# Attention heads turned another way: every second head of the last three chunks token-major, and the late modulation weights summed during the first output projection

## The chip, the cores and the metric

One NeuronCore of one Trainium2 chip runs the whole program. The metric is device time in microseconds (us) of one execution; less is better. The engines are named as the profile names them: PE is TensorE's matmul, PEld its weight load, DVE VectorE, ACT ScalarE, POOL GpSimd, SP the sync engine, which issues most DMAs. "SPq" and "ACTq" are rows of DMA issues on the queues of SP and ACT.

## The reference

One transformer layer with adaptive layer norm: 2048 tokens, width 1024, 32 query heads of 128 on 4 key/value heads, of whose 2048 keys only the last 512 are seen, and a gated FFN of width 3584. All tensors are bf16.

```
mod = silu(c) @ w_mod                      -> six rows of 1024: sa, ca, ga, sb, cb, gb
h = layernorm(x) * (1 + ca) + sa
q = h @ wq;  s = q k^T / sqrt(128)         # k, v: the last 512 positions of the caches
o = softmax(s) @ v;  x = x + ga * (o @ wo)
h = layernorm(x) * (1 + cb) + sb
x = x + gb * ((silu(h @ w_gate) * (h @ w_up)) @ w_down)
```

## The kernel before

**Tiling.** The tokens are four chunks of 512 (`CH`), each of four tiles of 128. Attention runs chunk by chunk, 32 heads in each, so 128 heads in all, numbered `i`; after the last head of a chunk comes that chunk's output projection, `oproj` (eight pieces `k` of 32 matmuls, in turn into PSUM banks `QB` and `XB`); the last chunk's is spread over the loop's end. The FFN follows, chunk by chunk. Layer norms are generators (`ln_task`) that `run_bg` advances one step per head; their DMA turns put the normalized rows feature-major into `hT`.

**Order.** One recording layer, `T.op` (L55), emits every instruction in program order and adds the semaphore waits that its buffers need, so each engine runs its instructions in the order of the loop at L903, and a wait holds up all that stands behind it on its engine. Nearly every matmul has line L271.

**One head before.** In iteration `i` stand: `qproj(i+3)`, eight 128x512 matmuls into bank `QB`, which DVE copies to a `qT` slot (CAST, L644); `scores(i-1)`, four 128x512 matmuls with the keys stationary, so that a score tile has keys on its partitions, into banks 0 to 3, and two `Exp` of 1024 columns on ACT (L813) into one of two `ex` slots; `pv(i-2)`, sixteen 128x129 matmuls with a piece of the probabilities stationary and the values moving, their 129th column a column of ones that gives the row sums, into banks 5 and 6. DVE then takes the reciprocals (L831), scales the 128x512 result (L834), and SP turns it by DMA (L837, "o-turn" below) into the head's row of `oT_all`, which `oproj` reads. SP also loads 1 MB of `wq` for every four heads (`load_wq`, L357).

**The late weights.** 24 columns of `mod` (sb, cb and gb) are wanted only in the FFN. `load_mt(n)` (L588) loads 128 columns of `w_mod` turned by DMA, `mod_col(n)` (L593) multiplies them by silu(c) and sums along the row on DVE. Before, one of each stands at every 9/4 heads from head 34 on, through chunk 1 and into chunk 2, with two buffers.

**Names.** `resid` (L853, L855) multiplies a finished PSUM bank by the gate and adds it to `x_res`, both on DVE; `oproj_end` calls it. `mod_take` and `mod_gain` copy finished columns to where `modulate` reads them.

Of the kernel before, what the change touches and what calls it, by code (L numbers as in the profile page):

```python
# [3 lines left out]
ALU = mybir.AluOpType  # L4
AF = mybir.ActivationFunctionType
BF16 = mybir.dt.bfloat16
# [124 lines left out]
def bass_adaLN_cond__sliding_block_cached__swiglu_ffn__prompt_kernel(  # L131
# [44 lines left out]
    def dq(name, issuer=None):  # L176
        return T.stream(name, nc.alloc_semaphore(name), issuer or nc.sync, inc=16)
# [44 lines left out]
    def bank(b, n=512, off=0):  # L222
        return ps[:, b * 512 + off:b * 512 + off + n]
# [19 lines left out]
    B_mv = [_Buf("mv%d" % i) for i in range(4)]  # L243
    B_rs = [_Buf("rs%d" % i) for i in range(4)]
    B_rl = [_Buf("rl%d" % i) for i in range(2)]
    B_ns = [_Buf("ns%d" % i) for i in range(2)]
    B_tmp = [_Buf("tmp%d" % i) for i in range(2)]
    B_h2 = [[_Buf("h2_%d_%d" % (s, dt)) for dt in range(DT)] for s in range(2)]
# [12 lines left out]
    with nc.Block() as block:  # L261

        @block.gpsimd
        def _(g):
# [5 lines left out]
            def mm(out_ap, lhsT, rhs, start, stop, reads, bank_buf, skip=False):  # L270
                T.op(PE, lambda: TE.matmul(out_ap, lhsT, rhs, start=start, stop=stop, skip_group_check=skip),  # L271
                     reads=reads, writes=[bank_buf])
# [145 lines left out]


            B_ns4 = B_ns + [_Buf("ns2"), _Buf("ns3")]  # L420
            nsc4 = [t[:, :] for t in nsc] + [arena.at(OFF_EX + (4 + 2 * i) * KB, [D], BF16, [B_ns4[2 + i]]) for i in range(2)]
# [154 lines left out]

            NF = NE + DT
            NL = NJ - NF
            B_mt = [_Buf("mt%d" % i) for i in range(2)]
            mt = [arena.at(OFF_H20 + (2 + 2 * i) * KB, [D], BF16, [B_mt[i]]) for i in range(2)]  # L580
            sc_row = arena.at(OFF_H20 + 6 * KB, [D], BF16, [B_scr])
            Q_mt = [dq("q_mt%d" % i) for i in range(2)]

            def load_mt(n):
                if n < 2:
                    for b_ in B_qT[NQT:]:
                        B_mt[n].absorb(b_)
                T.op(Q_mt[n % 2], lambda: SP.dma_start_transpose(  # L588
                    mt[n % 2].rearrange("p (a b) -> p a b", a=1), w_mod[:, (NF + n) * P:(NF + n + 1) * P]),
                     writes=[B_mt[n % 2]])  # L590

            def mod_col(n):
                T.op(DVE, lambda: V.scalar_tensor_tensor(mt[n % 2], mt[n % 2], 1.0, sc_row, op0=ALU.mult, op1=ALU.mult,  # L593
                                                         accum_out=mcol[:, n:n + 1]),
                     reads=[B_scr], writes=[B_mt[n % 2], B_mcol])
# [150 lines left out]
            for dt in range(DT):  # L746
                shift(dt)

            B_ex = [_Buf("ex%d" % i) for i in range(NEX)]
            ex_s = [arena.at(OFF_EX + i * 4 * KB, [KT, CH], BF16, [B_ex[i]]) for i in range(NEX)]  # L750
# [54 lines left out]
            def scores(i):  # L805
                ch, h = divmod(i, Hq)
                gk = h // rep
                qs = q_slot(i)
                es = i % NEX
                for kt in range(KT):  # L810
                    mm(bank(SCB + kt), kT_sb[:, gk * KT + kt, :], qT_s[qs], True, True, [B_kT[gk], B_qT[qs]], PB[SCB + kt])
                for kp in range(KT // 2):
                    T.op(ACT, lambda: A.activation(ex_s[es][:, 2 * kp:2 * kp + 2, :], banks2(SCB + 2 * kp), AF.Exp, scale=att_scale),  # L813
                         writes=[PB[SCB + 2 * kp], PB[SCB + 2 * kp + 1], B_ex[es]])

            def pv(i):
                ch, h = divmod(i, Hq)
                gk = h // rep
                es = i % NEX
                os_ = i % NOS  # L820

                for jj in range(2):
                    for kt in range(KT):
                        for jb in range(2):
                            j = 2 * jb + jj
                            b = PVB + jb
                            mm(bank(b, P + 1, jj * 130), ex_s[es][:, kt, j * P:(j + 1) * P], v_aug[:, gk * KT + kt, 0:P + 1],
                               kt == 0, kt == KT - 1, [B_ex[es], B_va, B_vg[gk]], PB[b])
                both = [PB[PVB], PB[PVB + 1]]
                r = i % 2  # L830
                T.op(DVE, lambda: V.reciprocal(rl[r][:, :].rearrange("p (a b) -> p a b", a=2), psap(PVB * 512 + P, [[512, 2], [130, 2]])),  # L831
                     writes=both + [B_rl[r]])
# [4 lines left out]
                T.op(Q_tr[os_], lambda: SP.dma_start_transpose(oT_all[:, h, :].rearrange("p (j q) -> p j q", j=TPC),  # L837
                                                               o_s[os_].rearrange("p j d -> p (j d)")),
                     reads=[B_os[os_]], writes=[B_oT[h]])

            B_wo = [_Buf("wo%d" % i) for i in range(8)]
            wo_s = [None] * 8
# [15 lines left out]
            def oproj_mm(ch, k, b, h0, h1):  # L858
                j, hf = divmod(k, 2)
                for h in range(h0, h1):  # L860
                    mm(bank(b), oT_all[:, h, j * P:(j + 1) * P], wo_s[h // 4][:, h % 4, hf * 512:(hf + 1) * 512],
                       h == 0, h == Hq - 1, [B_wo[h // 4], B_oT[h]], PB[b])
# [33 lines left out]
            t2 = Hq + 6 + (9 * (NL - 1)) // 4  # L896
            TURNT = (28, t2 + 1)
            PUTT = {33: (0, c_sil, B_csil), 30: (1, mrow[0:DT, :], B_mrow), t2 + 3: (2, mrow[0:DT, :], B_mrow)}
            GETT = {35: (0, sc_row, B_scr), 31: (1, rowb[0][:, :], B_row[0]), t2 + 4: (2, rowb[1][:, :], B_row[1])}
            LOADT = {Hq + 2 + (9 * n) // 4: n for n in range(NL)}  # L900
            LOADO = {5 + (21 * p) // 8: p for p in range(8)}
            LOADK = {1: 1, 5: 2, 6: 3}
            for i in range(1, NA + 2):  # L903
                ch, h = divmod(i, Hq)
                if i in LOADK:
# [10 lines left out]
                    load_wo(LOADO[i])  # L916
                if i in GATET:
                    gate_turn(GATET[i])
                if i in TURNT:
                    if i > Hq:  # L920
                        T.op(DVE, lambda: V.tensor_copy(mstg[:, 0:DT], mcol[:, 2 * DT:3 * DT]), reads=[B_mcol], writes=[B_mstg])
                    row_turn()
                if i in PUTT:
                    row_put(*PUTT[i])
# [8 lines left out]
                if i + LEAD < NA:  # L933
# [9 lines left out]
                        qproj_mm(NQ0 + i // 2, QB, 0, HK)  # L943
                    else:
                        qproj(NQ0 - 1 + i // 2, QB, HK)
                if i - 4 in LOADT:
                    n = LOADT[i - 4]
                    mod_col(n)
                    g0, last = divmod(n, DT)
                    if last == DT - 1:  # L950
                        mod_take(g0, B_late[g0 + 1])
                        if g0 == 1:
                            mod_gain(1, B_late[2], B_g[1])
                n = i - (NA - LEAD)
                if 0 <= n <= 2:
                    oproj_mm(NCH - 1, 0, QB, 8 * n, 8 * n + 8)
                elif n >= 3:
                    oproj_mm(NCH - 1, 1, XB, 8 * (n - 3), 8 * (n - 3) + 8)
                if 1 <= i - 1 < NA:
                    scores(i - 1)  # L960
                if 0 <= i - 2 < NA:
                    pv(i - 2)
                    ch2, h2 = divmod(i - 2, Hq)
                    if i % 4 == 1 and i > 5:
# [166 lines left out]
```

## Time and profile before

| | us |
|---|---|
| median of 3 runs | 1270.56 |
| lowest, highest | 1270.37, 1270.61 |
| the profiled execution's own time | 1270.14 |
| its span, first to last instruction | 1268.3 |
| busy: PE, PEld, DVE | 1255.1, 640.7, 485.1 |
| busy: ACT, POOL | 341.6, 56.0 |

The granted TensorE clock stands at full speed over the span. In the page's slices the DMA engines are busiest in the first tenth; over the three later chunks of attention their mean busy share lies near a half. Head stages and output projections alternate: the first `oproj` runs from 139 to 193 us, chunk 1's heads follow it, and the FFN begins near 685 us.

### The profile page before, as it was taken

How to read it: one execution, taken by the hardware profiler on the slowest of the kernel's cores; microseconds unless marked ns; L12 is line 12 of the kernel's file. 1: busy time of each engine (PE TensorE's matmuls, PEld its weight loads, DVE VectorE, ACT ScalarE, POOL GpSimd, SP SyncE). 2: the span in 40 equal slices, each digit the busy share in tenths (PEclk: the TensorE clock that was granted, in tenths of full speed). 3: DMA queues.
4: the chain of work that ended last, by engine and by line, in shares of the span. 5: the costliest groups of instructions: out<-in, count | busy, mean ns of one | idle time of the engine just before them, and what ended most of it. 6: DMA issues, size and time to landing. Idle time of an engine off the chain costs nothing.

```text
span 1268.3 us, 17609 instructions
## 1 busy us (share of the span) xinstructions
PE 1255.1 (99%) x7442; PEld 640.7 (51%) x7583; DVE 485.1 (38%) x894; ACT 341.6 (27%) x389; POOL 56.0 (4%) x95
## 2 busy tenths in 40 slices
PE   8999999999999999999999999999999999999999
PEld 5655545555455554555544444444444444444444
DVE  4676226764257641365322321233212321222122
ACT  4655205553035550155510111011100111011100
POOL 1530000000000000000000000000000000000000
PEclk9999999999999999999999999999999999999999
DMA  9998306875029641064243972055512644034200
GB/s 320 264 263 218 92 1 127 177 171 125 1 57 177 138 114 34 9 129 123 61 145 100 291 246 94 25 158 150 168 40 72 177 141 134 17 128 154 67 9 25
DMA packets 239997, 156.67 MB, mean 124 GB/s; under 512 B 133296, under 2 KB 225840, under 8 KB 239920
## 3 DMA queue, kind: packets, MB, share of 16 engines
q1 hardware_dynamic: 181664, 96.83, 31.6%
q10 hardware_dynamic: 58256, 58.73, 14.6%
q8 instruction: 59, 0.97, 0.3%
q14 instruction: 18, 0.15, 0.1%
HBM read 119.93 MB, written 4.20 MB: 98 GB/s over the span
## 4 chain that ended last, share of the span: by engine, by line
PE 98%; issue 1%; DMA 0%; SPq 0%; DVE 0%
PE ps L271 98%; DMA arena<-in_w_mod_dram 0%; SPq L309 0%; SPq L334 0%; PE ps L275 0%; DVE arena L496 0%; DVE tmp L853 0%; DVE arena L855 0%; DVE gain_f L486 0%
## 5 line engine op out<-in xcount | busy, mean ns | idle before, releaser
L271 PE MATMUL ps<-arena 128*128 128x512 bf16 (+1 forms) x7213 | 1249.3, 333 | 10.1 <-POOL arena L298 2.0
L271 PEld LDWEIGHTS ps<-arena 128*128 128x128 bf16 x7354 | 632.9, 98 | 621.5 <-issue 2.1
L813 ACT ACTIVATE arena<-ps 128x1024 bf16<-128x1024 f32 x256 | 261.9, 1023 | 345.1 <-PE ps L271 333.4
L1059 ACT ACTIVATE arena<-ps 128x512 bf16<-128x512 f32 x112 | 66.9, 597 | 499.6 <-PE ps L271 499.6
L1060 DVE TENSOR_TENSOR arena<-ps,arena 128x512 bf16<-128x512 f32 x112 | 77.5, 692 | 276.2 <-PE ps L271 276.2
L853 DVE TENSOR_TENSOR tmp<-ps,rowb 128x512 f32<-128x512 f32 (+1 forms) x65 | 44.4, 683 | 318.8 <-PE ps L271 318.8
L644 DVE CAST arena<-ps 128x512 bf16<-128x512 f32 x120 | 82.8, 690 | 47.7 <-PE ps L271 47.7
L834 DVE TENSOR_TENSOR arena<-ps,rl 128x512 bf16<-128x512 f32 x128 | 88.5, 691 | 4.7 <-DVE rl L831 0.2
L831 DVE RECIPROCAL rl<-ps 128x4 f32<-128x4 f32 x128 | 23.4, 182 | 114.1 <-PE ps L271 114.1
L429 POOL TENSOR_SCALAR rstd<-mv 128x1 f32<-128x1 f32 x28 | 6.1, 216 | 910.3 <-DVE mv L428 910.3
L424 DVE BATCH_NORM_STATS2 st<-x_res 128x6 f32<-128x512 bf16 x62 | 42.4, 683 | 3.4 <-DMA x_res<-in_A_x_dram 3.3
L593 DVE SCALAR_TENSOR_TENSOR arena<-arena 128x1024 bf16<-128x1024 bf16 x24 | 29.2, 1215 | 0.0
L855 DVE TENSOR_TENSOR arena<-tmp,x_res 128x512 bf16<-128x512 f32 (+2 forms) x33 | 22.3, 677 | 1.1
L855 DVE TENSOR_TENSOR x_res<-tmp,x_res 128x512 bf16<-128x512 f32 x32 | 22.2, 693 | 1.1
L440 DVE TENSOR_SCALAR arena<-arena,gain,mod_bf 128x512 bf16<-128x512 bf16 x56 | 21.2, 420 | 0.0
L435 DVE TENSOR_SCALAR nsc<-x_res,mv,rstd 128x1024 bf16<-128x1024 bf16 x30 | 19.2, 641 | 0.0
L431 POOL TENSOR_TENSOR rstd<-rstd,mhalf 128x1 f32<-128x1 f32 x28 | 15.7, 559 | 2.3
L772 POOL TENSOR_SCALAR arena<-arena,sc_bf 128x512 f32<-128x512 bf16 x8 | 12.9, 1614 | 0.5 <-POOL arena L774 0.2
L774 POOL TENSOR_TENSOR arena<-arena 128x512 f32<-128x512 f32 x8 | 10.1, 1265 | 0.7
L428 DVE BATCH_NORM_AGGREGATE mv<-st 128x2 f32<-128x12 f32 x28 | 5.8, 209 | 1.0
L271 PEld LDWEIGHTS ps<-sc_bf,arena 128*128 128x128 bf16 x128 | 4.4, 96 | 1.4 <-DMA arena<-in_w_mod_dram 0.3
L271 PE MATMUL ps<-sc_bf,arena 128*128 128x1 bf16 x128 | 4.7, 164 | 0.3 <-DMA arena<-in_w_mod_dram 0.3
(56 smaller groups left out, 59.4 us busy)
## 6 DMA issues: line engine op xcount, KB each, us to landing
arena<-in_A_wq_dram SPq DMA_DIRECT2D x30, 1024.0 KB, 5.8
arena<-in_B_w_gate_dram ACTq DMA_DIRECT2D x28, 1024.0 KB, 5.4
arena<-in_B_w_up_dram ACTq DMA_DIRECT2D x28, 1024.0 KB, 7.9
arena<-in_A_wo_dram SPq DMA_DIRECT2D x8, 1024.0 KB, 7.6
arena<-in_B_w_down_dram SPq DMA_DIRECT2D x7, 1024.0 KB, 8.3
out_dram<-arena SPq DMA_DIRECT2D x15, 256.0 KB, 2.0
x_res<-in_A_x_dram SPq DMA_DIRECT2D x3, 1024.0 KB, 7.0
arena<-arena SPq DMA_TRANSPOSE x132, 2.6
```

What stands on the lines that cost most here:

```text
L271: T.op(PE, lambda: TE.matmul(out_ap, lhsT, rhs, start=start, stop=stop, skip_group_check=skip), reads=reads, writes=[bank_buf])
L424: T.op(DVE, lambda: V.bn_stats(st_[sl][:, hf * 6:hf * 6 + 6], x_res[:, t, hf * 512:hf * 512 + 512]), reads=[B_x[t]], writes=[B_st[sl]])
L440: T.op(DVE, lambda: V.tensor_scalar(dst[:, dt, :], dst[:, dt, :], gain[gi][:, dt:dt + 1], mod_bf[:, ccol + dt:ccol + dt + 1], op0=ALU.mult ...
L593: T.op(DVE, lambda: V.scalar_tensor_tensor(mt[n % 2], mt[n % 2], 1.0, sc_row, op0=ALU.mult, op1=ALU.mult, accum_out=mcol[:, n:n + 1]), rea ...
L644: T.op(DVE, lambda: V.tensor_copy(qT_s[qs], bank(b)), writes=[PB[b], B_qT[qs]])
L813: T.op(ACT, lambda: A.activation(ex_s[es][:, 2 * kp:2 * kp + 2, :], banks2(SCB + 2 * kp), AF.Exp, scale=att_scale), writes=[PB[SCB + 2 * k ...
L831: T.op(DVE, lambda: V.reciprocal(rl[r][:, :].rearrange("p (a b) -> p a b", a=2), psap(PVB * 512 + P, [[512, 2], [130, 2]])), writes=both + ...
L834: T.op(DVE, lambda: V.tensor_tensor(o_s[os_].rearrange("p (a b) d -> p a b d", a=2), psap(PVB * 512, [[512, 2], [130, 2], [1, P]]), rlb, A ...
L853: T.op(DVE, lambda: V.tensor_tensor(tmp[s][:, 0:n], bank(b, n), rowb[ri][:, c0:c0 + n], ALU.mult), reads=[B_row[ri]], writes=[PB[b], B_tmp ...
L855: T.op(DVE, lambda: V.tensor_tensor(dst[:, c0:c0 + n], tmp[s][:, 0:n], x_res[:, t, c0:c0 + n], ALU.add), reads=[B_tmp[s], B_x[t]], writes= ...
L1059: T.op(ACT, lambda: A.activation(sg_s[ss], bank(gb), AF.Silu), writes=[PB[gb], B_sg[ss]])
L1060: T.op(DVE, lambda: V.tensor_tensor(guT[:, ft, :], bank(ub), sg_s[ss], ALU.mult), reads=[B_sg[ss]], writes=[PB[ub], B_gu[ft]])
```

## The change

Two things change.

**Token-major heads.** `NAT` holds the even heads from 34 to 126, 47 of them. For these, `nat_scores` makes the four query tiles stationary and moves the keys, so that a score tile has tokens on its partitions. ACT runs four `Exp` of 512 columns, each with `accum_out`, the row sum. `nat_norm` takes reciprocals of the sums on DVE, two at a time, and scales four 128x512 pieces of probabilities in place. `nat_turn` turns the whole 128x2048 tile by one DMA into a slot `pt`. `nat_pv`, four iterations later, needs four 128x512 matmuls, the values stationary and the turned probabilities moving, which give the head's result feature-major; ACT copies it to `oT_all`. Such a head has no reciprocal, no scaling and no o-turn of its own after the matmuls. Its probabilities lie in `pn[0]`, the place of `ex` slot 0, or in `pn[1]`, the place of `tmp`; the heads between use `ex` slot 1, and head 32 uses `nsc`. At a seam between chunks the first such head is placed into `oproj`: its `nat_scores` after piece 0, its `nat_norm` after piece 1.

**Late weights.** `late_cols(k)` is called behind each of the eight pieces of the first `oproj` and holds three `mod_col` each, with four buffers in the place of `hT[0]`; behind the last piece it also holds the two `mod_take` and `mod_gain`. The loop has no `mod_col` any more.

In an odd iteration the order on PE is `qproj`, `nat_scores(i+1)`, `pv(i-2)`; in an even one `qproj`, `scores(i-1)`, `nat_pv(i-4)`. `load_wq` stands one iteration earlier, ahead of `nat_turn`.

```diff
-    nsc = [S_("nsc%d" % i, [P, D], BF16) for i in range(2)]
-    tmp = [S_("tmp%d" % i, [P, 512], F32) for i in range(2)]
+    psum = [S_("psum%d" % i, [P, 4], F32) for i in range(2)]
+    pinv = [S_("pinv%d" % i, [P, 4], F32) for i in range(2)]
+    nsc_t = S_("nsc", [P, 2 * D], BF16)
+    nsc = [nsc_t[:, i * D:(i + 1) * D] for i in range(2)]
+    tmp_t = S_("tmp", [P, 1024], F32)
+    tmp = [tmp_t[:, i * 512:(i + 1) * 512] for i in range(2)]
...
+            NMT = 4
+            L_ORDER = list(range(2 * DT, NL)) + list(range(2 * DT))
+            def load_mt(m):
+                sl = m % NMT
+                n = L_ORDER[m]
+                if mt[sl] is None:
+                    mt[sl] = arena.at(OFF_HT + 2 * sl * KB, [D], BF16, [B_mt[sl]])
...
+            def late_cols(k):
+                for m in range(3 * k, 3 * k + 3):
+                    mod_col(m)
+                    if m + NMT < NL:
+                        load_mt(m + NMT)
+                if k == 3:
+                    T.op(DVE, lambda: V.tensor_copy(mstg[:, 0:DT], mcol[:, 2 * DT:3 * DT]), reads=[B_mcol], writes=[B_mstg])
+                    row_turn()
+                if k == 4:
+                    row_put(2, mrow[0:DT, :], B_mrow)
+                if k == 5:
+                    row_get(2, rowb[1][:, :], B_row[1])
+                if k == 7:
+                    for g0 in range(2):
+                        mod_take(g0, B_late[g0 + 1])
+                    mod_gain(1, B_late[2], B_g[1])
...
+            NAT0 = Hq + 2
+            NAT = set(range(NAT0, NA, 2))
+            B_pn = [[_Buf("pn0_%d" % hf) for hf in range(2)], B_tmp]
+            pn = [None, tmp_t[:, :].bitcast(BF16)]
...
+            def ex_slot(i):
+                return NEX if i % Hq == 0 and i + 2 in NAT and i not in NAT else i % NEX
+            def p_slot(i):
+                return (i - NAT0) // 2 % 2
...
+            def nat_scores(i):
...
+                for j in range(TPC):
+                    mm(bank(SCB + j), qT_s[qs][:, j * P:(j + 1) * P],
+                       kT_sb[:, gk * KT:(gk + 1) * KT, :].rearrange("p a b -> p (a b)"), True, True,
+                       [B_kT[gk], B_qT[qs]], PB[SCB + j])
+                for j in range(TPC):
+                    T.op(ACT, lambda: A.activation(pn[s][:, j * 512:(j + 1) * 512], bank(SCB + j), AF.Exp, scale=att_scale,
+                                                   accum_out=psum[s][:, j:j + 1]),
+                         writes=[PB[SCB + j], B_pn[s][j // 2], B_psum[s][j // 2]])
+            def nat_norm(i, hf):
+                s = p_slot(i)
+                T.op(DVE, lambda: V.reciprocal(pinv[s][:, 2 * hf:2 * hf + 2], psum[s][:, 2 * hf:2 * hf + 2]),
+                     reads=[B_psum[s][hf]], writes=[B_pinv[s][hf]])
+                for j in (2 * hf, 2 * hf + 1):
+                    pj = pn[s][:, j * 512:(j + 1) * 512]
+                    T.op(DVE, lambda: V.tensor_scalar(pj, pj, pinv[s][:, j:j + 1], None, op0=ALU.mult),
+                         reads=[B_pinv[s][hf]], writes=[B_pn[s][hf]])
+            def nat_turn(i):
+                s = p_slot(i)
+                pt_of[i] = (pt[s], B_pt[s])
+                T.op(Q_pt[s], lambda: SP.dma_start_transpose(pt[s], pn[s]), reads=B_pn[s], writes=[B_pt[s]])
+            def nat_pv(i):
...
+                for kt in range(KT):
+                    mm(bank(PVB).rearrange("p (j q) -> p j q", j=TPC), v_aug[:, gk * KT + kt, 0:P], ptv[:, :, kt, :],
+                       kt == 0, kt == KT - 1, [B_va, B_vg[gk], pb], PB[PVB])
+                T.op(ACT, lambda: A.activation(oT_all[:, h, :], bank(PVB), AF.Copy), writes=[PB[PVB], B_oT[h]])
...
-            def oproj(ch):
+            def oproj(ch, between, last):
                 for k in range(2 * TPC):
                     b = [QB, XB][k % 2]
-                    oproj_mm(ch, k, b, 0, Hq)
+                    if k == 0:
+                        oproj_mm(ch, k, b, 0, Hq - 8)
+                        for n in last:
+                            nat_pv(n)
+                    oproj_mm(ch, k, b, 0 if k else Hq - 8, Hq)
                     oproj_end(ch, k, b)
+                    if k < len(between):
+                        between[k]()
+                    if ch == 0:
+                        late_cols(k)
...
-                if i - 4 in LOADT:
-                    n = LOADT[i - 4]
-                    mod_col(n)
...
+                if i % 4 == 0 and i > NAT0:
+                    load_wq(i // 4 + 2)
...
+                seam = (i - 1) % Hq == 0 and i + 1 in NAT
...
+                if i in NAT and (i - 2) % Hq:
+                    nat_norm(i, 1)
+                nat = i % 2 == 1 and i + 1 in NAT
+                if nat and not seam:
+                    run_bg(1)
+                    nat_scores(i + 1)
-                if 1 <= i - 1 < NA:
+                if 1 <= i - 1 < NA and i - 1 not in NAT:
                     scores(i - 1)
                 if 0 <= i - 2 < NA:
-                    pv(i - 2)
+                    if i - 4 in pt_of:
+                        nat_pv(i - 4)
+                    if i in NAT and (i - 2) % Hq:
+                        nat_turn(i)
+                    if i - 2 not in NAT:
+                        pv(i - 2)
+                    if nat and not seam:
+                        nat_norm(i + 1, 0)
...
                     if h2 == Hq - 1 and ch2 < NCH - 1:
-                        oproj(ch2)
-                run_bg(1)
+                        oproj(ch2, [lambda: nat_scores(i + 1), lambda: (nat_norm(i + 1, 0), nat_norm(i + 1, 1))],
+                              [n for n in sorted(pt_of) if n // Hq == ch2])
+                        if seam:
...
+                            nat_turn(i + 1)
...
-            load_wgu(0, B_oT[Hq - 2:])
-            load_wgu(1)
             HL = Hq - 4
             oproj_mm(NCH - 1, 1, XB, 16, HL)
+            for n in sorted(pt_of):
+                nat_pv(n)
+            load_wgu(0, B_oT[Hq - 1:])
+            load_wgu(1)
```

More of the change, by code (lines that the diff above doesn't have):

```diff
@@ L245, in bass_adaLN_cond__sliding_block_cached__swiglu_ffn__prompt_kernel @@
     B_rl = [_Buf("rl%d" % i) for i in range(2)]
+    B_psum = [[_Buf("psum%d_%d" % (i, hf)) for hf in range(2)] for i in range(2)]
+    B_pinv = [[_Buf("pinv%d_%d" % (i, hf)) for hf in range(2)] for i in range(2)]
     B_ns = [_Buf("ns%d" % i) for i in range(2)]
@@ L420, in _ @@
             B_ns4 = B_ns + [_Buf("ns2"), _Buf("ns3")]
-            nsc4 = [t[:, :] for t in nsc] + [arena.at(OFF_EX + (4 + 2 * i) * KB, [D], BF16, [B_ns4[2 + i]]) for i in range(2)]
+            nsc4 = nsc + [arena.at(OFF_EX + (4 + 2 * i) * KB, [D], BF16, [B_ns4[2 + i]]) for i in range(2)]
             def stats(t, sl, hf):
@@ L578, in _ @@
             NL = NJ - NF
-            B_mt = [_Buf("mt%d" % i) for i in range(2)]
-            mt = [arena.at(OFF_H20 + (2 + 2 * i) * KB, [D], BF16, [B_mt[i]]) for i in range(2)]
+            NMT = 4
+            B_mt = [_Buf("mt%d" % i) for i in range(NMT)]
+            mt = [None] * NMT
             sc_row = arena.at(OFF_H20 + 6 * KB, [D], BF16, [B_scr])
[L582 to L590, printed above, removed]
@@ L592, in mod_col @@
-            def mod_col(n):
-                T.op(DVE, lambda: V.scalar_tensor_tensor(mt[n % 2], mt[n % 2], 1.0, sc_row, op0=ALU.mult, op1=ALU.mult,
-                                                         accum_out=mcol[:, n:n + 1]),
-                     reads=[B_scr], writes=[B_mt[n % 2], B_mcol])
+            Q_mt = [dq("q_mt%d" % i) for i in range(NMT)]
+            L_ORDER = list(range(2 * DT, NL)) + list(range(2 * DT))
[4 more added lines that the diff above has]
+                    mt[sl] = arena.at(OFF_HT + 2 * sl * KB, [D], BF16, [B_mt[sl]])
+                T.op(Q_mt[sl], lambda: SP.dma_start_transpose(
+                    mt[sl].rearrange("p (a b) -> p a b", a=1), w_mod[:, (NF + n) * P:(NF + n + 1) * P]),
+                     writes=[B_mt[sl]])
@@ new lines, in mod_col @@
+            def mod_col(m):
+                sl = m % NMT
+                n = L_ORDER[m]
+                T.op(DVE, lambda: V.scalar_tensor_tensor(mt[sl], mt[sl], 1.0, sc_row, op0=ALU.mult, op1=ALU.mult,
+                                                         accum_out=mcol[:, n:n + 1]),
+                     reads=[B_scr], writes=[B_mt[sl], B_mcol])
+            def late_cols(k):
[14 more added lines that the diff above has]
+                    mod_gain(1, B_late[2], B_g[1])
+                    for b_ in B_hT[0]:
+                        for m_ in B_mt:
+                            b_.absorb(m_)
@@ L747, in _ @@
                 shift(dt)
-            B_ex = [_Buf("ex%d" % i) for i in range(NEX)]
-            ex_s = [arena.at(OFF_EX + i * 4 * KB, [KT, CH], BF16, [B_ex[i]]) for i in range(NEX)]
+            B_ex = [[_Buf("ex%d" % i)] for i in range(NEX)]
+            ex_s = [arena.at(OFF_EX + i * 4 * KB, [KT, CH], BF16, B_ex[i]) for i in range(NEX)]
+            B_ex.append(B_ns)
+            ex_s.append(nsc_t[:, :].rearrange("p (a b) -> p a b", a=KT))
             o_s = [arena.at(OFF_OS + i * 1 * KB, [TPC, P], BF16, [B_os[i]]) for i in range(NOS)]
@@ L808, in scores @@
                 qs = q_slot(i)
-                es = i % NEX
+                es = ex_slot(i)
                 for kt in range(KT):
                     mm(bank(SCB + kt), kT_sb[:, gk * KT + kt, :], qT_s[qs], True, True, [B_kT[gk], B_qT[qs]], PB[SCB + kt])
+                for b_ in B_pn[0] if es == 0 else ():
+                    B_ex[0][0].absorb(b_)
                 for kp in range(KT // 2):
                     T.op(ACT, lambda: A.activation(ex_s[es][:, 2 * kp:2 * kp + 2, :], banks2(SCB + 2 * kp), AF.Exp, scale=att_scale),
-                         writes=[PB[SCB + 2 * kp], PB[SCB + 2 * kp + 1], B_ex[es]])
+                         writes=[PB[SCB + 2 * kp], PB[SCB + 2 * kp + 1]] + B_ex[es])
             def pv(i):
@@ L818, in pv @@
                 gk = h // rep
-                es = i % NEX
+                es = ex_slot(i)
                 os_ = i % NOS
@@ L827, in pv @@
                             mm(bank(b, P + 1, jj * 130), ex_s[es][:, kt, j * P:(j + 1) * P], v_aug[:, gk * KT + kt, 0:P + 1],
-                               kt == 0, kt == KT - 1, [B_ex[es], B_va, B_vg[gk]], PB[b])
+                               kt == 0, kt == KT - 1, B_ex[es] + [B_va, B_vg[gk]], PB[b])
                 both = [PB[PVB], PB[PVB + 1]]
@@ L839, in pv @@
                      reads=[B_os[os_]], writes=[B_oT[h]])
+            NAT0 = Hq + 2
+            NAT = set(range(NAT0, NA, 2))
+            B_pn = [[_Buf("pn0_%d" % hf) for hf in range(2)], B_tmp]
+            pn = [None, tmp_t[:, :].bitcast(BF16)]
+            B_pt = [_Buf("pt%d" % s) for s in range(2)]
+            pt = [None, None]
+            pt_of = {}
+            Q_pt = [dq("q_pt%d" % i) for i in range(2)]
+            def ex_slot(i):
+                return NEX if i % Hq == 0 and i + 2 in NAT and i not in NAT else i % NEX
@@ new lines, in p_slot, with pt_region @@
+            def p_slot(i):
+                return (i - NAT0) // 2 % 2
+            def pt_region(off):
+                for s in range(2):
+                    B_pt[s] = _Buf("pt%d" % s)
+                    pt[s] = arena.at(off + s * 4 * KB, [TPC * KT, P], BF16, [B_pt[s]])
+            def nat_scores(i):
+                gk = i % Hq // rep
+                qs = q_slot(i)
+                s = p_slot(i)
+                for b_ in B_pn[0] if s == 0 else ():
+                    b_.absorb(B_ex[0][0])
+                if pn[0] is None:
+                    pn[0] = arena.at(OFF_EX, [TPC * KT * P], BF16, B_pn[0])
+                for j in range(TPC):
[6 more added lines that the diff above has]
+                         writes=[PB[SCB + j], B_pn[s][j // 2], B_psum[s][j // 2]])
@@ new lines, in nat_turn @@
+            def nat_turn(i):
+                s = p_slot(i)
+                pt_of[i] = (pt[s], B_pt[s])
+                T.op(Q_pt[s], lambda: SP.dma_start_transpose(pt[s], pn[s]), reads=B_pn[s], writes=[B_pt[s]])
+            def nat_pv(i):
+                h = i % Hq
+                gk = h // rep
+                s = p_slot(i)
+                pa, pb = pt_of.pop(i)
+                ptv = pa.rearrange("p (j k) q -> p j k q", j=TPC)
+                for kt in range(KT):
+                    mm(bank(PVB).rearrange("p (j q) -> p j q", j=TPC), v_aug[:, gk * KT + kt, 0:P], ptv[:, :, kt, :],
+                       kt == 0, kt == KT - 1, [B_va, B_vg[gk], pb], PB[PVB])
+                T.op(ACT, lambda: A.activation(oT_all[:, h, :], bank(PVB), AF.Copy), writes=[PB[PVB], B_oT[h]])
@@ L895, in _ @@
             GATES = {26: 0, 27: 1}
[L896 to L900, printed above, removed]
+            PUTT = {22: (0, c_sil, B_csil), 30: (1, mrow[0:DT, :], B_mrow)}
+            GETT = {25: (0, sc_row, B_scr), 31: (1, rowb[0][:, :], B_row[0])}
+            LOADT = {30: 0, 31: 1, 32: 2, 33: 3}
             LOADO = {5 + (21 * p) // 8: p for p in range(8)}
             LOADK = {1: 1, 5: 2, 6: 3}
+            PTAT = {NAT0: OFF_H20, 3 * Hq: OFF_HT}
             for i in range(1, NA + 2):
@@ L918, in _ @@
                     gate_turn(GATET[i])
-                if i in TURNT:
-                    if i > Hq:
-                        T.op(DVE, lambda: V.tensor_copy(mstg[:, 0:DT], mcol[:, 2 * DT:3 * DT]), reads=[B_mcol], writes=[B_mstg])
+                if i == 28:
                     row_turn()
@@ L945, in _ @@
                         qproj(NQ0 - 1 + i // 2, QB, HK)
-                if i - 4 in LOADT:
-                    n = LOADT[i - 4]
-                    mod_col(n)
[L949 to L953, printed above, removed]
+                if i % 4 == 0 and i > NAT0:
+                    load_wq(i // 4 + 2)
                 n = i - (NA - LEAD)
@@ L958, in _ @@
                     oproj_mm(NCH - 1, 1, XB, 8 * (n - 3), 8 * (n - 3) + 8)
-                if 1 <= i - 1 < NA:
+                seam = (i - 1) % Hq == 0 and i + 1 in NAT
+                if i + 1 in PTAT and not seam:
+                    pt_region(PTAT[i + 1])
+                if i in NAT and (i - 2) % Hq:
[5 more added lines that the diff above has]
+                if 1 <= i - 1 < NA and i - 1 not in NAT:
                     scores(i - 1)
                 if 0 <= i - 2 < NA:
-                    pv(i - 2)
+                    if i - 4 in pt_of:
[6 more added lines that the diff above has]
+                        nat_norm(i + 1, 0)
                     ch2, h2 = divmod(i - 2, Hq)
-                    if i % 4 == 1 and i > 5:
+                    if i % 4 == 1 and 5 < i < NAT0:
                         load_wq((i + 4) // 4 + 1)
@@ L968, in _ @@
                     if h2 == Hq - 1 and ch2 < NCH - 1:
-                        oproj(ch2)
-                run_bg(1)
+                        oproj(ch2, [lambda: nat_scores(i + 1), lambda: (nat_norm(i + 1, 0), nat_norm(i + 1, 1))],
+                              [n for n in sorted(pt_of) if n // Hq == ch2])
+                        if seam:
+                            if i + 1 in PTAT:
+                                pt_region(PTAT[i + 1])
+                            nat_turn(i + 1)
+                if not nat or seam:
+                    run_bg(1)
                 for n in GATEP.get(i, ()):
```

## The prediction

> **What bounds the kernel now.** I read the page first: busy time, then the chain that ended last.
>
> ```profile
> PE 1255.1 (99%) x7442; PEld 640.7 (51%) x7583; DVE 485.1 (38%) x894; ACT 341.6 (27%) x389; POOL 56.0 (4%) x95
> PE 98%; issue 1%; DMA 0%; SPq 0%; DVE 0%
> ```
>
> PE is the bound throughout; no other engine holds the end. So only fewer PE microseconds, or fewer pauses of PE, can gain, and every new wait of PE is lost in full. What a matmul costs start to start is read from the chain in order of time (start, length, what):
>
> ```profile
> 138.11 10.74 PE ps L271 x49
> 148.90 10.74 PE ps L271 x49
> ```
>
> Fifty matmuls of 512 columns, one that joins the pieces included, take 148.90 - 138.11 = 10.79 us: 0.2158 us each. DVE's timeline over the end of the first output projection gives the head's period and the order at the seam:
>
> ```profile
> 194.07 0.69 DVE L855 TENSOR_TENSOR x_res<-tmp,x_res 128x512 bf16<-128x512 f32 x1
> 195.07 0.69 DVE L644 CAST arena<-ps 128x512 bf16<-128x512 f32 x1 [0.31 <-PE ps L271]
> 196.84 0.18 DVE L831 RECIPROCAL rl<-ps 128x4 f32<-128x4 f32 x1 [1.08 <-PE ps L271]
> ...
> 198.57 0.69 DVE L644 CAST arena<-ps 128x512 bf16<-128x512 f32 x1 [0.22 <-PE ps L271]
> 200.34 0.18 DVE L831 RECIPROCAL rl<-ps 128x4 f32<-128x4 f32 x1 [1.08 <-PE ps L271]
> ```
>
> A head takes 200.34 - 196.84 = 3.50 us. Twelve 512-column matmuls are 2.59 of it, so the sixteen of 129 columns take 0.91 us, 0.057 each. The sum of the matmuls is the whole period: heads have no pause that could be removed.
>
> **What PE saves.** A token-major head has four 512-column matmuls, 0.863 us, for those sixteen; the scores keep four. It saves 0.91 - 0.863 = 0.047 us, times 47 heads: **-2.2 us**. This is all that the change can gain. [...]
>
> **What the late weights add at the seam.** Off the heads they take 24 sums of DVE and 24 turns of SP; the cover there was PE's own work, so this gains nothing. In the first `oproj` a piece lasts 32 x 0.2158 = 6.9 us and DVE has `resid` (2 x 0.69) and three sums in it, so pieces 0 to 6 hide them; with `nat_norm`, piece 1 is about full, and a bank is wanted again only a piece later. Behind the last piece nothing hides them. A sum costs, from the timeline near 405 us:
>
> ```profile
> 404.79 1.22 DVE L593 SCALAR_TENSOR_TENSOR arena<-arena 128x1024 bf16<-128x1024 bf16 x1
> 405.31 2.18 SPq L454 DMA_TRANSPOSE arena<-nsc  x1
> 405.93 0.08 DVE L593 DVE_READ_ACCUMULATOR arena<-arena 128x1 f32 x1
> ```
>
> It ends 1.22 us after its start and the next one waits for that end, 0.03 us as between L853 and L855: 1.25. By the built order DVE's queue after the last piece is `resid`, three sums, two `mod_take`, `mod_gain`, and only then the CAST of `qproj(37)`, which frees `QB`, the only bank of the q projection. `resid` ends at 194.76. The sums end at 194.79 + 3 x 1.25 = 198.54, three copies of 0.17 make it 199.05, the CAST 199.75. PE is ready for `qproj(38)` at 196.6 (eight matmuls ahead of the CAST at 198.57, which starts 0.42 after the last of them begins) and goes on at 199.8. **+3.15 us**, once; 2.8 if the sums overlap by the 1.16 us in which a free successor follows, 3.8 if each takes 1.3 and the waits of PE 0.2 more. DVE then catches up; iteration 36 has neither `pv` nor `nat_pv`, so PE is 0.9 us shorter there and can wait again: 0 to 0.3, I take **+0.15**.
>
> **What hides the rest.** Per two heads PE has 6.95 us; count from the start of the odd iteration.
> - ACT: the four `Exp` start 0.42 us after the first score matmul, at 2.15. An ACT row of 512 columns from PSUM lasts 597 ns; the row that reads the accumulator 187. With two waits of 0.05, 4 x 0.784 + 0.1 = 3.24, until 5.4. The last bank is wanted at 5.88: 0.4 us of cover. From above, an ACT row with bias and accumulator took 1148 ns where an `Exp` of as many columns takes 1023; 125 more on each uses the cover and costs 0.1 a pair. I take nothing. The heads between (2.14 us) and the copy of `nat_pv` (0.60) fit behind it.
> - DVE: two CASTs 1.38, one head's reciprocal and scaling 0.87, two small reciprocals, and four products at 0.35 (L675, one operation) to 0.42 (L440, two): about 4.2 of 6.95, the norm's tasks 0.7 to 1.5 at times. `nat_norm`'s second half ends at about 7.0 at the latest. Nothing.
> - The turn of 128x2048 is not in the trace. Its issue and landing are bounded by the rows for smaller ones (last column: median to landing):
>
> ```profile
> arena<-arena SPq DMA_TRANSPOSE x132, 2.6
> arena<-nsc SPq DMA_TRANSPOSE x28, 5.1
> arena<-in_w_mod_dram SPq DMA_TRANSPOSE x24, 4.3
> ```
>
> The first is nearly all 128x512, the others are twice that. A straight line through 2.6 and 5.1 gives 10.1 us for four times. From below: where no load stands ahead, the nsc turn lands in 3.1 (its minimum), so 0.5 more per 512 columns, 4.1. I take 5 to 6, since the short rows are the nearest without a queue. Who waits: `nat_pv`, 14 us after the turn's issue; and, earlier, the `Exp` of head `i+4`, which overwrites the same `pn`, at 2.15 + 13.9 = 16.1 against an issue at 7.0. Cover 9.1 us. SP's issue of the nsc turn is 1.23 at best, 2.2 to 2.7 behind a load; if it is 2 to 4 for the big one, four heads ask 2 x 4 + 2 x 1.19 + 0.53 + 1.1 = 12 of SP's 13.9 us. Nothing.
> - At `i = 40` SP issues the load of x and that of `wq` (7.0 and 5.8 us to landing) straight ahead of the turn: all three one after the other land 0 to 2 us after the cover ends. **+0.5**, between 0 and 2.
> - The seams of chunks 1 and 2 carry no sums; `nat_scores` and `nat_norm` there lie beside 55 us of `oproj`. `load_wq` one iteration earlier and `load_wgu` behind the last `nat_pv` are issued many us before use. Nothing.
>
> Sum: -2.2 + 3.15 + 0.15 + 0.5 = **+1.6**. The profiled execution took 1270.14 (span 1268.3 and 1.8 around it), so 1271.7; it lies 0.4 below the median, so beside the median **1272.1**. With the bounds, +0.6 to +3.9: 1271.2 to 1274.5.
>
> **Rivals.**
> 1. The pause cools PE. At the start, cold, twelve 512-column matmuls took:
>
> ```profile
> 3.10 4.34 PE L271 MATMUL ps<-arena 128*128 128x512 bf16 x12
> ```
>
> against 2.59 warm. If the seam's pause makes PE cold again, 1.75 us come on top: 1273.9. It decides when the pause outlasts what the clock forgives. [...] No pause of this length is in the trace. Chance 0.10.
> 2. The turns bind. At 10.1 us the same `pn` comes free 1.0 late in every four heads: 23.5 times 1.0, 1296. For it: the straight line. Against: the 3.1. It decides at 9.1 us, or when a turn's issue passes 5 us and fills SP's queue. Chance 0.11.
> 3. ACT binds: 47 x 0.1, 1277, if an `Exp` with its row sum passes 0.9 us. Chance 0.09.
> 4. Faster: the seam's pause is absent and the saving alone stays, 1268.4. It needs three sums in 0.65 us (199.75 back to 196.6); the rows say 3.75. Chance 0.04, counting 0.01 for heads bound by the weight load (98 ns a row in PEld; sixteen would be 1.57, 33 us to gain), which the 3.50 us period excludes.
>
> **How the numbers follow.** The forecast has 0.66. A measurement tells 0.2% from no change, 2.5 us: below 1268.0 is faster, above 1273.1 slower. Rivals 1 to 3 (0.30) are slower, and of the forecast the part with a long pause or the collision at 40, 0.12: slower 0.42. The rest of the forecast and nearly all of rival 4 are the same: 0.56; faster 0.02. The range takes in the forecast, rivals 1 and 3 and, below, half of a smaller pause: 1269.6 to 1280; rivals 2 and 4 stay out, 0.15.
>
> **What would show it.** L831-to-L831 over two heads at 6.95; one gap of PE of about 3.1 us near 197, released by DVE's CAST, with three L593-like sums ahead of it; ACT rows of 512 columns near 0.6; turns landing under 9 us. PE gaps that repeat in every pair, released by ACT or by a DMA, would prove me wrong, and so would a lower granted clock or wider matmul spacing after the pause.

## The result and the profile after

The changed kernel takes 1273.77 us (median of 16 executions, 1272.19 to 1275.54) against 1270.49 of the kernel before (1270.03 to 1270.80): ratio 1.0025, 95% interval 1.0017 to 1.0033. The executions differ more than those of before, and the granted clock mostly goes with it: ten stand at 0.999 (1273.12 to 1275.54), six at 1.000 (1272.19 to 1273.05, and one of 1274.44). The profiled one took 1273.79, span 1271.9, 3.6 above that of before, clock 0.999.

The page's busy line and chain, as shown of before:

```profile
PE 1263.1 (99%) x7019; PEld 617.1 (49%) x7019; DVE 518.9 (41%) x1081; ACT 392.7 (31%) x718; POOL 55.9 (4%) x95
PE 98%; DVE 1%; DMA 0%; issue 0%; ACT 0%; DVEq 0%; ACTq 0%
```

PE is still the bound, but DVE now has 1% of the chain: a piece of DVE that PE waits for. The waits of PE name it (in total, times, longest), and DVE's timeline at the end of the first output projection shows it:

```profile
PE ps L277 <- DVE arena L675: 3.1, 2, 2.9
```

```profile
195.15 0.69 DVE L952 TENSOR_TENSOR x_res<-tmp,x_res 128x512 bf16<-128x512 f32 x1
195.75 1.22 DVE L604 SCALAR_TENSOR_TENSOR arena<-arena 128x1024 bf16<-128x1024 bf16 x1
...
197.09 1.23 DVE L604 SCALAR_TENSOR_TENSOR arena<-arena 128x1024 bf16<-128x1024 bf16 x1
...
198.42 1.23 DVE L604 SCALAR_TENSOR_TENSOR arena<-arena 128x1024 bf16<-128x1024 bf16 x1
...
199.69 0.24 DVE L629 CAST mod_bf<-mcol 128x8 bf16<-128x8 f32 x2
199.97 0.17 DVE L478 TENSOR_SCALAR gain<-mod_bf 128x8 bf16<-128x8 bf16 x1
200.05 0.68 DVE L675 CAST arena<-ps 128x512 bf16<-128x512 f32 x1
```

Three late sums and three small copies stand ahead of the CAST of `qproj(37)`. PE has to wait for it (PE's timeline, two windows of it):

```profile
196.81 1.07 PE L277 MATMUL ps<-arena,nsc 128*128 128x129 bf16 x16
200.79 3.51 PE L277 MATMUL ps<-arena 128*128 128x512 bf16 x8 [2.91 <-DVE arena L675]
```

The sixteen matmuls of 129 columns are through at 196.81 + 16 x 0.057 = 197.72; PE goes on at 200.79, a pause of 3.07 us. Then eight matmuls take 3.51 us from the first's start to the last's end; at full clock they take 7 x 0.216 + 0.38 = 1.89 (0.38 is one matmul from start to end, 10.74 - 48 x 0.2158 in the chain of before). So 1.6 us more are lost, and the granted clock (column after POOL) says why:

```profile
core 0: us, PE busy (x) PEld busy (x) DVE busy (x) ACT busy (x) POOL busy (x), PEclk, DMA share, GB/s
190.00:197.90 7.90, 7.88 (x49) 3.93 (x47) 5.88 (x11) 1.23 (x2) 0.00 (x0) 1.00 0.73 150
200.95:204.36 3.41, 3.41 (x10) 1.17 (x9) 1.22 (x3) 0.00 (x0) 0.00 (x0) 0.54 0.20 38
204.40:212.00 7.60, 7.44 (x55) 4.03 (x54) 6.17 (x15) 5.64 (x13) 0.79 (x2) 1.00 0.33 81
```

For 3.4 us behind the pause the clock is about half: 0.54 over that window, and the trace's record has 0.50 for 3.413 us, from 200.67 to 204.08. Everywhere else the heads run as planned. Two L866 rows of DVE, one pair of heads apart:

```profile
400.42 0.18 DVE L866 RECIPROCAL rl<-ps 128x4 f32<-128x4 f32 x1 [0.48 <-PE ps L277]
...
407.37 0.18 DVE L866 RECIPROCAL rl<-ps 128x4 f32<-128x4 f32 x1 [0.62 <-PE ps L277]
```

6.95 us where two heads of before took 7.00.

The sum of the profiled execution: saving -2.2, pause 3.07, slow matmuls 1.6, and PE's small gaps of 0.38 (at 45, in chunk 0, the second of the two waits for a CAST above; what held it up was not looked into), 0.33 (at 208), 0.37 (at 235) and 0.13 (at 309) and twice 0.09 at the later seams: 3.9, against 3.6 measured. The two agree within 0.3 us.

### The profile page after: what moved, and what is told of

Its sections match the earlier page's. It is cut to its first block, busy times and chain, and to the rows that moved or that the text cites. A ratio compares the mean times of both kernels' runs of the same rounds, so it can differ in the third digit from the quotient of the medians.

```text
span 1271.9 us, 17309 instructions
## 1 busy us (share of the span) xinstructions
PE 1263.1 (99%) x7019; PEld 617.1 (49%) x7019; DVE 518.9 (41%) x1081; ACT 392.7 (31%) x718; POOL 55.9 (4%) x95
## 4 chain that ended last, share of the span: by engine, by line
PE 98%; DVE 1%; DMA 0%; issue 0%; ACT 0%; DVEq 0%; ACTq 0%
PE ps L277 98%; DVE st L430 0%; DVE arena L604 0%; DMA x_res<-in_A_x_dram 0%; DVE arena L869 0%; PE ps L281 0%; DVE arena L675 0%; ACT tmp L909 0%; DVE arena L701 0%; DVE tmp L950 0%; DVE nsc L441 0%; DVE tmp L919 0%; DVE x_res L952 0%; DVE mv L530 0%; DVE rl L866 0%
## 5 line engine op out<-in xcount | busy, mean ns | idle before, releaser
L277 PEld LDWEIGHTS ps<-arena 128*128 128x128 bf16 x6774 | 608.4, 98 | 648.7 <-issue 5.3
L848 ACT ACTIVATE arena<-ps 128x1024 bf16<-128x1024 f32 x160 | 163.7, 1023 | 229.9 <-PE ps L277 222.5
L1179 ACT ACTIVATE arena<-ps 128x512 bf16<-128x512 f32 x112 | 66.9, 597 | 501.0 <-PE ps L277 498.1
L675 DVE CAST arena<-ps 128x512 bf16<-128x512 f32 x120 | 82.8, 690 | 77.9 <-PE ps L277 77.9
L909 ACT ACTIVATE arena<-ps 128x512 bf16<-128x512 f32 x96 | 56.9, 595 | 26.3 <-PE ps L277 21.9
L909 ACT ACTIVATE tmp<-ps 128x512 bf16<-128x512 f32 x92 | 54.5, 595 | 25.8 <-PE ps L277 21.6
L869 DVE TENSOR_TENSOR arena<-ps,rl 128x512 bf16<-128x512 f32 x81 | 56.0, 691 | 3.0 <-DVE rl L866 0.2
L866 DVE RECIPROCAL rl<-ps 128x4 f32<-128x4 f32 x81 | 14.7, 182 | 73.9 <-PE ps L277 73.9
L919 DVE TENSOR_SCALAR arena<-arena,pinv 128x512 bf16<-128x512 bf16 x96 | 33.9, 353 | 3.4
L936 ACT ACTIVATE arena<-ps 128x512 bf16<-128x512 f32 x47 | 27.8, 592 | 19.6 <-PE ps L277 19.6
L919 DVE TENSOR_SCALAR tmp<-tmp,pinv 128x512 bf16<-128x512 bf16 x92 | 32.5, 353 | 3.3
L909 ACT ACTIVATION_READ_ACCUMULATOR arena<-ps 128x1 f32 x96 | 18.9, 197 | 0.0
```

The source lines that it names most:

```text
L675: T.op(DVE, lambda: V.tensor_copy(qT_s[qs], bank(b)), writes=[PB[b], B_qT[qs]])
L909: T.op(ACT, lambda: A.activation(pn[s][:, j * 512:(j + 1) * 512], bank(SCB + j), AF.Exp, scale=att_scale, accum_out=psum[s][:, j:j + 1]), ...
L919: T.op(DVE, lambda: V.tensor_scalar(pj, pj, pinv[s][:, j:j + 1], None, op0=ALU.mult), reads=[B_pinv[s][hf]], writes=[B_pn[s][hf]])
L1179: T.op(ACT, lambda: A.activation(sg_s[ss], bank(gb), AF.Silu), writes=[PB[gb], B_sg[ss]])
```

## The experiments

Theory A: the heads bring their 2.2 us, and the sums behind the last piece cost a pause and, by execution, a slow clock. Theory B: the heads themselves cost, by turns or ACT. All kernels were timed in five rounds beside the kernel before, on three chips: the first four, then the mended kernel and its runs with two and three sums, then the run with four sums and the three at the end. The kernel before took 1270.50, 1270.41 and 1270.43 there; on the third chip it spread more, 1269.88 to 1272.28, with one of 27 executions at clock 0.999.

**Which half loses.** First, no sum behind the last piece; the 24 sums stand 4, 2, 4, 4, 4, 3, 3, 0 behind the eight pieces:

```diff
-                for m in range(3 * k, 3 * k + 3):
+                for m in range(sum(SUMS[:k]), sum(SUMS[:k + 1])):   # SUMS = [4, 2, 4, 4, 4, 3, 3, 0]
...
-                if k == 7:
+                if k == 6:
                     for g0 in range(2):
```

> The 24 late sums are spread 4, 2, 4, 4, 4, 3, 3, 0 over the eight pieces of the first output projection, so that none stands behind the last piece; the heads stay as in the change. Theory A (the seam's pause, 3.1 us, and the cold clock behind it, 1.7 us, are what the change loses): no PE gap over 0.5 us near 197, clock 1.000, and the saving of 2.2 us stays but for about 0.5 of small waits: 1.7 us below the kernel before, near 1268.8, ratio 0.9987. Theory B (the token-major heads themselves cost, by their turns or ACT): the time stays 1 to 3 us above the kernel before.

Measured: 1269.60, ratio 0.9993 (0.9984 to 1.0002), clock 1.000 in all. The pause is gone and theory A holds in direction, but the median is 0.8 above its number and the executions spread from 1268.82 to 1271.15. Its profile, of one of the quickest executions (1268.97), shows gaps of 0.46 at 230, 0.18 at 204, 0.15 at 120 and 0.13 at 304; what holds up the slower executions is in no profile.

Second, the other half alone, no token-major head:

```diff
-            NAT = set(range(NAT0, NA, 2))
+            NAT = set()
```

Two lines go with it: no place is kept for turned probabilities, and nothing of a token-major head is put into `oproj`.

> No token-major head at all; only the late sums are moved to the first output projection, three behind each piece. Theory A: PE pauses 3.1 us behind the last piece and loses 1.7 more where the clock falls: 3.1 to 4.8 us above the kernel before, 1273.6 to 1275.3, the clock 1.000 or 0.999 by execution. Theory B: within 1 us of the kernel before.

Measured: 1275.60, ratio 1.0042 (1.0029 to 1.0054). The profiled execution, 1273.75, has the pause (2.9 us of wait for the CAST) and kept its clock; the others stand at 0.997 to 0.999 and at 1275.6 and more, a little over theory A's upper end. Of that, 0.3 lies outside the span: its executions take 2.1 us more than their spans, those of the kernel before 1.8. Theory B falls by the two kernels together: the loss is there without a single token-major head, and with the heads but without the sums behind the last piece there is none.

**Is it the clock?** The change with thirteen matmuls in the pause whose results nobody reads:

```diff
+                    if i == Hq + 2:
+                        for _ in range(13):
+                            mm(bank(XB), kT_sb[:, 0, :], kT_sb[:, 0:KT, :].rearrange("p a b -> p (a b)"), True, True,
+                               [B_kT[0]], PB[XB])
```

> The change as it is, and thirteen matmuls of 512 columns whose results nobody reads, 2.8 us of PE, placed where PE pauses (behind the values' matmuls of head 32). They need nothing that is late, so they lie in the pause and keep PE busy. If the clock behind the pause is what makes the executions differ: clock 1.000 in all, none of the eight slow matmuls, near 1272.1 in all, 1.6 below the change's median, and a spread under 1 us. If contention of DMAs makes them differ: the same median and spread as the change (1272.2 to 1275.5).

Measured: 1272.76, ratio 1.0021 (1.0012 to 1.0030), clock 1.000 in all, no slow matmuls. The median fell by 1.0, not 1.6, and the spread stayed (1272.39 to 1275.27). So the clock is one cause of the long times, and the spread has another. The chain of this profile, of a slow execution (1274.07), shows one:

```profile
114.21 7.78 DMA arena<-in_A_wq_dram
121.99 0.05 issue
122.03 2.12 PE ps L277 x9
```

In chunk 0 PE waits 1.1 us for a load of `wq` that lands 7.8 us after its issue (before: 5.5 for the same load). Ahead of it on SP's queue stands the 256 KB fetch of silu(c) as a row, which the change issues at head 25 instead of 35. Nearer the end the same profile has two gaps that make 0.91 near 235, where the change's has 0.37.

**The load of x.** The gap near 235 had the loads of x and `wq` at head 40 ahead of a turn. Moved to head 33, on the kernel without sums behind the last piece:

```diff
-            LOADX = {19: 2, 40: 3}
+            LOADX = {19: 2, 33: 3}
```

> As the kernel with no sum behind the last piece, and the load of the last chunk of x moved from head 40 to head 33, ahead of the first output projection. If the gap near 235 comes from that load and the load of wq standing ahead of a turn, it goes: 0.3 to 0.5 us less than without this move, near 1268.4; if not, the same time and the gap stays.

Measured: 1273.24, ratio 1.0024 (1.0015 to 1.0032): 3.6 worse, not better. The gap near 230 is gone, but SP's timeline (start, length of the issue) and then the chain show what I had put behind the load:

```profile
140.15 0.58 SPq L308 DMA_DIRECT2D x_res<-in_A_x_dram  x1
140.78 1.20 SPq L874 DMA_TRANSPOSE arena<-arena  x1
```

The chain of the same moments (start, length, what it is):

```profile
140.15 0.58 SPq L308
140.73 0.04 issue
140.78 6.97 DMA arena<-arena
147.75 0.05 issue
147.79 4.21 PE ps L277 x11
```

Right behind the 1 MB load on SP's queue stands the o-turn of head 31, the last that the first piece of `oproj` needs; it lands after 6.97 us instead of 2.5 as in the change, PE waits 2.7 us, and the clock falls: eight of eleven executions stand below 1.000.

**The mended kernel.** No sum behind the last piece, silu(c) fetched at head 32, x loaded in the second output projection, where SP issues it at 307 and nothing behind it until 323:

```diff
-            GETT = {25: (0, sc_row, B_scr), 31:
+            GETT = {32: (0, sc_row, B_scr), 31:
...
-            LOADX = {19: 2, 40: 3}
+            LOADX = {19: 2}
...
+                    if ch == 1 and k == 2:
+                        load_x(3)
```

> The change with three placements mended: no late sum behind the last piece of the first output projection; the load of silu(c) as a row (256 KB) issued at head 32 instead of 25, out of chunk 0's crowded queue; the last chunk of x loaded behind the third piece of the second output projection. Theory: the variable wait near 120 (for wq, 0 to 1.1 us), the pause near 197 and the gap near 235 all go, and what is left is the saving of 2.2 us less about 0.3: 1268.6, ratio 0.9985, all executions within 0.6 us. Rival (the spread comes from the 47 turns): median near 1269.6 and a spread of 2 us, as with the first kernel that has no sum behind the last piece.

Measured: **1268.35**, 1268.09 to 1269.33, ratio 0.9986 (0.9977 to 0.9995): 2.1 faster than before, and faster than both kernels. PE's gaps in chunks 1 to 3 are 0.18 at 204, 0.13 at 304 and twice 0.09. DVE's timeline at the seam is that of before again, the CASTs 3.50 apart:

```profile
195.28 0.69 DVE L954 TENSOR_TENSOR x_res<-tmp,x_res 128x512 bf16<-128x512 f32 x1
196.28 0.69 DVE L677 CAST arena<-ps 128x512 bf16<-128x512 f32 x1 [0.31 <-PE ps L277]
...
199.78 0.69 DVE L677 CAST arena<-ps 128x512 bf16<-128x512 f32 x1 [0.22 <-PE ps L277]
```

**Pause and clock, on the mended kernel.** The number of sums behind the last piece sets the pause:

```diff
+            SUMS = [3, 3, 3, 3, 3, 3, 4, 2]
```

> The mended kernel with two late sums behind the last piece. Pause of PE 3.1 - 1.34 = 1.75 us. If the clock falls only with a pause of about 3 us: clock 1.000 in every execution, 1268.6 + 1.75 = 1270.4, spread under 0.6. If any pause of over a microsecond can lower it: some executions 1.7 us longer at 0.999.

```diff
+            SUMS = [3, 3, 3, 3, 3, 3, 3, 3]
```

> The mended kernel with three late sums behind the last piece, as in the change: pause 3.1 us. 1268.6 + 3.1 = 1271.7 where the clock stays and 1273.4 where it falls, two groups of executions about 1.7 us apart, the longer ones at clock 0.999. If the clock does not matter: one group at 1271.7.

The same with the thirteen unread matmuls of above in the pause:

> The mended kernel with three late sums behind the last piece and thirteen matmuls that nobody reads (2.8 us) in the pause. If the clock behind the pause makes the two groups: one group at 1271.7 to 1272.0, clock 1.000 in all, no slow matmuls. If not: the same as without them.

```diff
+            SUMS = [3, 3, 3, 3, 3, 3, 2, 4]
```

> The mended kernel with four late sums behind the last piece: pause 3.1 + 1.34 = 4.4 us. If the clock falls with long pauses: it falls in every execution, 1268.35 + 4.4 + 1.7 = 1274.5, all at 0.999, spread under 1 us. If the fall is chance, as often as with three: two groups, 1272.8 and 1274.5.

Measured (pause: start to start of PE's matmuls around it, less the 0.057 of the one before; the last row is from the third chip):

| sums behind the last piece | pause us | median us | lowest, highest | executions under clock 1.000 | ratio to before |
|---|---|---|---|---|---|
| none | 0 | 1268.35 | 1268.09, 1269.33 | 0 of 11 | 0.9986 |
| two | 1.74 | 1270.66 | 1270.20, 1272.53 | 0 of 11 | 1.0003 |
| three | 3.07 | 1273.31 | 1271.69, 1274.15 | 8 of 9 | 1.0023 |
| three, filled | filled | 1271.82 | 1271.33, 1272.51 | 0 of 11 | 1.0011 |
| four | 4.41 | 1275.06 | 1274.73, 1276.25 | 5 of 5 | 1.0037 |

The windows of the pause and behind it, with three sums unfilled (first two rows), filled (next two) and with four:

```profile
197.80:200.60 2.80, 0.00 (x0) 0.00 (x0) 2.63 (x9) 0.79 (x1) 0.00 (x0) 1.00 0.00 0
201.16:204.56 3.40, 3.40 (x10) 1.20 (x9) 1.28 (x3) 0.06 (x1) 0.00 (x0) 0.54 0.20 39
```

```profile
197.80:200.60 2.80, 2.80 (x18) 1.26 (x15) 2.63 (x8) 1.02 (x1) 0.00 (x0) 1.00 0.00 0
201.16:204.56 3.40, 3.40 (x29) 2.08 (x28) 2.65 (x5) 1.36 (x5) 0.04 (x1) 1.00 0.20 39
```

```profile
203.93:207.33 3.40, 3.40 (x18) 1.75 (x17) 1.50 (x3) 1.78 (x6) 0.59 (x2) 0.55 0.20 39
```

Unfilled, ten matmuls of 512 columns stand in the 3.4 us (in the change's trace they start 0.427 apart at the low clock: 201.19 to 203.75 in six steps); filled, the 29 are twelve of 512 columns, 0.216 apart, sixteen of 129 and one that was under way. The clock is 0.54 against 1.00, and nothing else was changed but that PE had unread work in the pause: 1.5 us between the medians. This shows the clock's part. Two sums give the pause without the clock: +2.3, of which the pause is 1.74 and the gap behind it 0.15 (0.33 instead of 0.18); the rest is not accounted for. Four give both every time.

Why three sums lower the clock in some executions only, no run shows. Of the three pauses, the one of 1.74 us came with a lower clock in 0 of 11 executions, the one of 3.07 in 22 of 30 (8 of 9, 10 of 16 of the change, and 4 of 5 with the sums alone), the one of 4.41 in 5 of 5; the kernel with x at head 33, whose profile has a wait of 2.7, stood below 1.000 in 8 of 11.

**What the two other mendings are worth.** Each alone, on the kernel without sums behind the last piece, the diffs as above:

> No late sum behind the last piece, and of the two other mendings only that the row of silu(c) is fetched at head 32 instead of 25; x is loaded at head 40 as in the change. If the early fetch made the variable wait for wq near 120: that wait is gone, 1268.35 + 0.5 for the gap near 230: 1268.8, spread under 1 us. If not: 1269.6 as without it.

> No late sum behind the last piece, and of the two other mendings only that the last chunk of x is loaded in the second output projection; silu(c) is fetched at head 25 as in the change. The gap near 230 is gone; if the wait near 120 comes from the fetch, it stays in some executions: median 1268.7 to 1269.3, spread 1 to 2 us.

Measured: the fetch alone 1269.90 (1268.60 to 1274.41), ratio 0.9998 (0.9989 to 1.0006); x alone 1269.02 (1268.28 to 1270.01), ratio 0.9988 (0.9979 to 0.9996). Moving x is worth 0.6 by the medians, but the two ratios' intervals overlap. Moving the fetch was not worth what I expected: its profile has no wait near 120, but one of 0.42 near 145, again for the o-turn of head 31, 0.30 near 106, and 0.72 near 231 at the load of x. Two of its executions stand at clock 0.999; neither was profiled. The profile with x moved alone keeps the wait near 121 (0.6 by the waits). So the early fetch and that wait go together: of the six profiles with the fetch at head 25 four have a gap near 120, 0.15 to 1.24 from start to start, and of the seven with it at head 32 none. Three of those seven have a gap of 0.13 to 0.42 near 144 instead, where the fetch now stands not far ahead of head 31's o-turn. What the fetch costs the median is not settled, all the less as these two kernels ran on the third chip and the one they are set beside on the first; both moves together are worth 1.25 (1269.60 to 1268.35), and all eleven executions of the mended kernel lie below the other's median.

**Are the 2.1 us the heads' own?** The mended kernel without token-major heads (edited as above):

> The late sums in the first output projection with all three mendings, and no token-major head. If the 47 heads alone bring the 2.1 us that the mended kernel gains: the kernel before's time, 1270.4, within 0.3. If taking the sums out of the heads brings part of it: lower by that part.

Measured: 1270.82, ratio 1.0002 (0.9994 to 1.0011). Moving the sums gains nothing by itself; the 47 heads are worth 1270.82 - 1268.35 = 2.5 us. By the median spans it is 1268.7 - 1266.5 = 2.2, as summed in the prediction: without token-major heads the time outside the span is 2.2 us, with them 1.8. Why, no profile shows.

## Why the prediction was right or wrong

The range and the direction hold: 1272.1 forecast, 1273.77 measured, which is 0.26% over before and, against the 0.2% that the text set, on the slower side by a little. That the range holds says little, since it was drawn up to 1280 for ACT. The likeliest case was not the commonest one. It fits the executions that kept their clock, 1272.19 to 1273.05 but for one; rival 1, 1273.9 at a chance of 0.10, fits the ten of sixteen that did not, and the median. A lower granted clock after the pause was among the signs that would prove the forecast wrong, and it came.

- The saving, -2.2: right; 6.95 us a pair, and 2.2 by the spans (2.5 by the times) between kernels that differ in the heads alone.
- The pause, +3.15: right at 3.07. A sum costs 1.34 (195.75 to 197.09), not 1.25; the copies overlap more than I let them (from the first, at 199.69, to the CAST, at 200.05, are 0.36 us, not 0.51).
- **The step that failed: rival 1's weight.** The chance of 0.10 rested on no measurement: no pause of that length was in the trace of before, and no row showed that one of 3.15 would leave the clock alone. The runs showed otherwise: with 3.07 the clock fell in 8 of 9 executions of the mended kernel and in 10 of 16 of the change. The price, 1.75 from the start of before (4.34 against 2.59), came out near, at 1.6; the sum behind it set 4.34 us up to the last matmul's end against 2.59 from start to start, and from start to end the warm twelve take 11 x 0.216 + 0.38 = 2.75, which leaves 1.59. In the change's trace PE works at 0.50 of the clock from 200.79 to 204.08, and half of these 3.29 us is 1.6.
- DVE's arrears behind the pause, +0.15: the gap is 0.33, just above the bound of 0.3, but 0.18 of it stays in the mended kernel, with no sum behind the last piece; what the pause adds is 0.15.
- The load of x at head 40, +0.5: 0.37 in the change's profile and, with the load moved, 0.6 less by the medians. The way was as told: the turn behind the two loads, issued at 223.4, is the one that took 9.6 us, past the cover of 9.1, and the `Exp` that overwrites its source starts at 233.03, as it lands.
- A term that was missing: the row of silu(c), fetched ten heads earlier into chunk 0's crowded queue. I costed the moves of `load_wq` and `load_wgu` and passed over this DMA; the wait for `wq` that shows with it is 0 in the change's profile, 0.6 and 1.1 in two others.
- The turns (rival 2): right. L925's rows give issues of 1.9 and 4.5 us (medians of its two sources) and landings of 4.2 to 9.6, median 6.0, where I took 5 to 6 against a cover of 9.1. Only the turn behind the loads at head 40 passed the cover, and its issue, 7.5 us, was the longest. The page's rows of the same kind as before:

```profile
arena<-arena SPq DMA_TRANSPOSE x109, 3.9
arena<-tmp SPq DMA_TRANSPOSE x23, 6.9
```

The first row mixes o-turns with 24 of the big turns; the second is big turns alone.

- ACT (rival 3): right, and with more room. The first and the last of a head's four `Exp`, and the read of its accumulator:

```profile
259.99 0.60 ACT L909 ACTIVATE tmp<-ps 128x512 bf16<-128x512 f32 x1 [0.61 <-PE ps L277]
...
262.12 0.60 ACT L909 ACTIVATE tmp<-ps 128x512 bf16<-128x512 f32 x1
...
262.62 0.19 ACT L909 ACTIVATION_READ_ACCUMULATOR tmp<-ps 128x1 f32 x1
```

From 259.99 to 262.81 are 2.8 us, not 3.24, since an accumulator's read overlaps the row before it (it starts at 262.62, that row ends at 262.72). The products took 353 ns, as line L675 of the kernel before said (348).
- Rival 4: out; the pause is in every profile with three sums that nothing fills. Its 0.65 us should read 0.60 (3.75 - 3.15).

## What to carry to other kernels

Where PE is the bound and a change saves a few hundredths of a microsecond a head, look at the seams first: side work put behind the last piece of a block delays the next block's first eviction, and one such place took more (a pause of 3.07 us) than 47 heads gave (2.2). Spread side work so that its last part ends before the block does, and count a PE pause of about three microseconds at nearly five where the clock falls (3.07 + 1.6 here), with a chance of its own for that (22 of 30 executions). List every DMA that is moved with what stands behind it on its queue: a 1 MB load ahead of a small urgent turn cost 2.7 us of PE.

## What the runs showed of the hardware

With a pause of PE of 1.74 us the clock never fell (0 of 11 executions), with one of 3.07 mostly (8 of 9; in the change 10 of 16), with one of 4.41 always (5 of 5); with the three microseconds filled with matmuls that nobody read it never did (0 of 11, and 0 of 11 in the change). In the change's trace the low clock, 0.50, stood for 3.413 us, with matmuls of 512 columns 0.427 us apart instead of 0.216; behind the pauses of 3.07 and 4.41 of the mended kernel the clock was 0.54 and 0.55 over 3.40 us. Without sums behind the last piece it fell now and then on the third chip: in one of 27 executions of the kernel before, one of 11 without token-major heads and two of 11 with the fetch moved alone. With four sums two executions stand at 0.997; two stretches like the change's would give that (2 x 3.413 x 0.50 of 1274 us is 0.003, an estimate), but neither execution was profiled. Some long executions at clock 1.000 are not explained: 1274.44 of the change, and 1275.27 with the pause filled.
